# A hand-written task order replaced by another: first weight tiles, chunk steps and up-projections of a fused SSD and bilinear FFN kernel interleaved anew

## The chip, the cores and the metric

The kernel runs on one core of a Trainium2 chip. The metric is the device time of one execution in microseconds; lower is better. Before the change three runs took 272.69, 273.26 and 274.73 us, a median of 273.26. Engine names in profile rows: PE is TensorE's matmuls and PEld its weight loads, DVE is VectorE, ACT is ScalarE, POOL is GpSimd, SP is SyncE, whose queue (SPq) issues the DMA transfers.

## The reference

Two stages follow each other. The first is a chunked state-space scan over 4 batches, 8 heads, 768 positions, head size 32 and state size 16; the second is a bilinear feed-forward network on its 3072 output rows of 256.

```python
for c in range(nc):                       # chunks along the sequence
    cum = np.cumsum(la, axis=-1)          # la = log(clip(a))
    L = np.exp(cum[..., :, None] - cum[..., None, :]) * causal
    M = np.einsum('bhin,bhjn->bhij', Cc, Bc) * L
    y = np.einsum('bhij,bhjd->bhid', M, xc) \
      + np.einsum('bhin,bhnd->bhid', Cc, state) * np.exp(cum)[..., None]
    state = exp(sum(la)) * state + sum_j(B_j x_j * exp(cum_last - cum_j))
...
a = x @ w1; b = x @ w2                    # x: 3072 x 256, w1, w2: 256 x 1024
h = (a * b) @ w3                          # w3: 1024 x 1024
out = h @ w_out                           # w_out: 1024 x 256
```

The weights and inputs are 64-bit floats in memory; the kernel reads them as pairs of 32-bit words.

## The kernel before, in words

The kernel cuts the sequence into 16 chunks of 48 positions. It forms w3 @ w_out once (1024 x 256, the tile `wo`), so that the network is two up-projections, their product, and one down-projection. Every operand of a large matmul is split into a high and a low half of reduced precision, and three matmuls (high by high, high by low, low by high) stand for one.

Nothing is scheduled by a compiler. A string, PLAN (L25), is the order of all 986 tasks, and the program is emitted by walking it: each word is a task's name, an engine letter behind a colon where there is a choice (V is DVE, S is ACT, G is POOL, D is the SP queue), and behind an @ the PSUM banks (there are eight) that it writes. Each engine runs its own tasks in the order in which they stand in the string, and waits where an operand is not there or a buffer is not free. So the order of two tasks of one engine, the choice of engine and the choice of banks are all that PLAN sets. `+8@7` means eight matmuls on zeros into bank 7.

The tasks, by name:

- `t.*`, `a.*`, `k.*`, `j.*`: the decays. `t.D` and `a.D` load log-decay inputs, `t.clip`, `t.ln`, `a.clip`, `a.ln`, `a.scan`, `a.hi`, `a.lo` work them up, `a.save` writes the running sums to DRAM (tile `cq`), `k.D1` and `k.D2` load constants (tile `gs`, from in_Bt), `k.L`, `k.R0`, `k.R1` cast them into the matmul operands `ld` and `rd`, `j.m` is a small matmul.
- `cN.X`, `cN.N`, `cN.B`, `cN.K`: the loads of chunk N: its x, its B, its B and C laid out for the matmul (tile `bc`), and from chunk 2 on its running sums (`ld<-cq`, `rd<-cq`). 
- `cN.Y0`, `cN.Y1` (chunks 0 and 1 alone) build decay operands from `k.D1` and `t.D`; `cN.D0`, `cN.D1` are the decay matmuls (three matmuls each in chunks 0 and 1, one each in chunks 2 to 7; later chunks use `F` and `G` steps on DVE or POOL instead); `E0`, `E1` their exponentials on ACT; `W0`, `W1` a product on POOL.
- `cN.CB` (L352): 32 small matmuls (`ps<-bc`), C by B. `cN.M0`, `cN.M1` multiply them by the decays on DVE (`r<-ps,r`), two banks each. `cN.MX` (L366): 64 small matmuls (`ps<-r,xe`), the chunk's output and next state at once. `cN.T` (L380) transposes the state on DVE (tile `z`), eight copies `cN.Z0` to `cN.Z7` carry it into the next chunk's operand `xe`, and `cN.hi`, `cN.lo` write the output as high and low half (tile `xT`), which the up-projections read. So chunk N+1's MX waits for all of chunk N's Z.
- `wJ.*`, `vHK.*`, `oJ.*`: weight tiles: J of w1 and w2 together, of w3 transposed, of w_out. `D` loads into one of four buffers `st`, `A` (ACT), `L` and `S` (DVE) make 32-bit floats out of the 64-bit ones (`mag`), `H` casts the high half and `P` subtracts to get the low half (L424 to L461). `vHK.M` is 12 matmuls toward `wo`, `eHI.a` and `eHI.b` copy `wo` out.
- `lS.F.m`: the up-projection of rows slice S (slices of 384, 384, 512, 512, 512, 512, 256 columns) for weight tile F: 12 matmuls into two banks; `a` copies the first bank (ACT), `g` multiplies by the second (DVE), `h` and `l` split the product. `dS.T.m`: 24 matmuls of the down-projection, `y` copies them out, `x` stores them.

Slice 0 needs chunks 0 and 1, slice 1 chunks 2 and 3, and so on, so the scan and the network are interleaved on PE. Helper lines that appear in the profile: all matmuls have L136, all loads L139, two-operand DVE and POOL work L142, copies L148, activations L151.

Of the kernel before, what the change touches and what calls it, by code (L numbers as in the profile page):

```python
# [33 lines left out]
l0.6.m@6,7 c2.Z4:S c2.Z3:G c3.M1:V w7.A:S v00.D c2.Z7:G c3.M0:V o0.D c2.Z5:G c2.Z6:G l0.5.g:V l0.6.a:S c2.Z2:V w7.L:V w1.A:S l0.4.m@0,4 c6.N w1.L:V
c4.N w7.S:V c2.Z1:V c5.B w7.H:S w1.S:V l0.4.a:S w7.P:G l0.6.g:V v10.D c3.MX@2,3 l0.4.g:V o1.D c4.D0@5 a.keep c3.hi:S c3.T:V c4.D1@6 w1.H:V l0.7.m@1,0
c4.E0:S c3.Z6:G c3.lo:V c3.Z1:S w1.P:G v00.A:S c4.E1:S c3.Z7:S c3.Z5:V c3.Z2:S c3.Z0:G l1.1.m@7,4 c3.Z4:S v00.L:V c3.Z3:S o0.L:V o0.A:S c5.K v00.S:V
l0.7.a:S c4.W1:G l1.1.a:S l0.7.g:V c4.W0:G l0.1.m@5,2 v00.H:S l1.1.g:V v00.P:V l0.1.a:S o0.S:V v10.A:S v10.L:V v01.D c4.CB@0,1,6,7 l0.1.g:V l1.6.m@3,4
o0.H:S v10.S:V o0.P:G c4.M0:V v10.H:S c6.B c4.M1:V o1.A:S v11.D v02.D l1.6.a:S o1.L:V c5.D0@5 c5.D1@2 v10.P:G c5.X l1.6.g:V c4.MX@0,1 c5.E0:S c6.K
c5.E1:S c5.CB@3,4,6,7 c4.hi:S c4.T:V c5.W0:G l1.4.m@5,2 c4.lo:V c5.W1:G c6.X c5.M0:V v01.A:S c7.B c5.M1:V v01.L:V l1.4.a:S o1.S:V c9.K l1.0.m@0,1
v01.S:V o1.H:S l1.4.g:V l1.0.a:S o1.P:V v11.A:S v11.L:V l1.3.m@3,4 v01.H:V v11.S:V l1.3.a:S v01.P:V v13.D v11.H:S v02.L:V l1.5.m@6,7 c4.Z6:S v12.D  # L40
c4.Z1:G l1.0.g:V c4.Z3:S c4.Z4:G o2.D l1.3.g:V c4.Z5:S v11.P:G v02.A:S c7.N c8.K l1.5.a:S c4.Z7:V c6.D1@5 c4.Z0:V l1.7.m@2,0 c4.Z2:V c6.E1:S c8.N
v02.S:V c6.W1:G l1.5.g:V l1.7.a:S c9.F0:V v04.D c9.F1:V c5.MX@3,4 c9.G0:G l1.7.g:V c6.CB@1,2,5,6 c5.hi:S c5.T:V c7.X l1.2.m@7,0 v13.A:S c5.Z7:V c8.B
c5.Z2:G c5.lo:V c5.Z3:G c5.Z6:S c6.M1:V c5.Z4:S c9.G1:G c5.Z5:S c5.Z0:S v12.A:S v12.L:V c6.D0@3 v13.L:V c5.Z1:S v00.M@4,5,-1,-1 l1.2.a:S c7.K v12.S:V
c6.E0:S v13.S:V o2.A:S v10.M@6,7,-1,-1 c6.W0:G l1.2.g:V v02.H:S c6.M0:V v02.P:V v03.D c6.MX@0,1 c8.F0:V v05.D v12.H:V v01.M@4,5,-1,-1 c9.N c6.hi:S
o2.L:V c6.hj:S v12.P:V c6.lo:V v04.A:S c8.X o2.S:V l2.6.m@3,2 v13.H:V o3.D o2.H:V v13.P:V l2.6.a:S o2.P:V v04.L:V v02.M@4,5,-1,-1 c8.G0:V v04.S:V
c8.E0:S v03.A:S c8.W0:G c6.T:V v06.D v11.M@6,7,-1,-1 l2.6.g:V c6.Z4:G c6.Z2:S c6.Z1:S c6.Z7:G c6.lp:V c6.Z3:G v03.L:V v05.A:S l2.0.m@3,2 v05.L:V
v03.S:V v05.S:V v03.H:S v07.D v04.H:V l2.0.a:S v14.D v03.P:V v04.P:V v03.M@4,5,-1,-1 o3.A:S o3.L:V c6.Z5:V o3.S:V v12.M@6,7,-1,-1 c8.F1:V v17.D
v06.A:S v06.L:V o3.H:V v06.S:V v04.M@4,5,-1,-1 v05.H:S o3.P:V v16.D v07.A:S v07.L:V v13.M@6,7,-1,-1 v05.P:V v07.S:V v14.A:S v14.L:V v15.D
v05.M@4,5,-1,-1 c8.G1:V v06.H:S v14.S:V v07.H:S c8.E1:S v06.P:V c7.D1@0 l2.1.m@1,3 v14.H:S c10.K c8.W1:G l2.0.g:V c7.E1:S v14.P:G v17.A:S c11.N
v16.A:S v07.P:V l2.1.a:S c7.W1:G v06.M@4,5,-1,-1 l2.1.g:V v15.A:S v16.L:V v15.L:V v14.M@6,7,-1,-1 c6.Z6:V v15.S:V c10.F1:G v15.H:S v07.M@4,5,-1,-1  # L50
v15.P:V c6.Z0:V v16.S:V l2.5.m@2,0 e01.a:S@5 v17.L:V e00.a:S@4 v16.H:V v17.S:V l2.5.a:S v16.P:V v17.H:S e00.b:V@4 v17.P:G c7.D0@1 v15.M@6,7,-1,-1
e01.b:V@5 c7.E0:S l2.5.g:V c7.W0:G c7.CB@1,2,3,4 c10.G1:V c10.N v16.M@6,7,-1,-1 c10.F0:V c9.B c7.M0:V c10.G0:G c7.M1:V c7.MX@0,1 c8.CB@2,3,4,5 c9.E0:S
c7.T:V c9.X v17.M@6,7,-1,-1 c9.E1:S c7.Z7:V c10.B c7.Z1:G c8.M0:V c7.Z3:S c9.W0:G c11.K c7.Z6:S c8.M1:V c7.Z0:G c7.Z5:S c7.Z2:S c7.Z4:G c7.hi:S
c9.W1:G l2.3.m@2,3 e10.a:S@6 l0.3.h:V c12.N l0.5.h:V e11.a:S@7 l0.3.l:G c7.lo:V l0.6.h:S e10.b:V@6 l1.0.h:S l0.1.h:V l0.2.h:S l0.5.l:V l0.7.h:S
l0.2.l:G e11.b:V@7 l2.7.m@4,5 l2.3.a:S l2.3.g:V l0.7.l:G l2.7.a:S l1.0.l:V l0.1.l:V l2.4.m@0,1 l1.2.h:V c11.F0:V l1.2.l:G l2.7.g:V l2.4.a:S l0.0.h:V
c11.G0:G l2.2.m@6,7 l2.4.g:V l0.0.l:G l0.6.l:V l2.2.a:S c11.F1:V l0.4.h:V c9.CB@2,3,4,5 l1.1.h:V l0.4.l:V c8.MX@0,1 c11.B c9.M1:V d0.1.m@6 l1.1.l:V
c10.E0:S c10.X c8.T:V c10.E1:S c10.W0:G l2.2.g:V c8.Z2:S c8.Z7:G c12.K c8.Z4:S c10.W1:G c9.M0:V c8.Z1:S c8.Z0:G c8.Z5:S c13.N c8.hi:S c8.Z6:V c8.Z3:V
c11.G1:V c8.lo:V c10.CB@2,3,4,5 d0.1.y:V c9.MX@0,1 c10.M1:V c12.B d0.1.x c10.M0:V d0.2.m@7 c11.E1:S c11.X c9.T:V c11.E0:S c11.W1:G c9.Z7:S c9.Z6:V
c13.K c9.Z0:G c9.hi:S c9.hj:S c9.Z2:V c9.Z5:G c9.lo:V c9.lp:V c9.Z3:G c9.Z1:V c9.Z4:G c12.F0:G c10.MX@4,5 d0.2.y:V d0.2.x c11.CB@0,1,2,3 c11.W0:G
c10.hi:S c10.T:V c12.X c12.G0:G l3.7.m@6,7 c10.Z4:S c10.lo:V c13.B c10.Z1:S c10.Z0:S c11.M1:V c14.N c10.Z3:G c12.E0:S c11.M0:V c10.Z5:G c12.W0:G  # L60
l3.7.a:S c10.Z2:V c12.F1:G l3.1.m@4,5 c10.Z6:V c12.G1:G l3.7.g:V c10.Z7:V c12.E1:S c13.F0:G l3.1.a:S c14.K c13.F1:G c11.MX@2,3 l3.1.g:V c12.CB@0,1,6,7
# [611 lines left out]
```

## Time and profile before

| | before |
|---|---|
| median of 3 runs | 273.26 us |
| profiled execution | 273.01 us |
| span of its instructions | 270.8 us |
| PE busy | 264.0 us, 97% |
| DVE busy | 173.0 us, 64% |
| ACT busy | 115.6 us, 43% |
| POOL busy | 81.5 us, 30% |
| matmuls, weight loads | 3022 each |
| DMA moved | 33.94 MB, mean 125 GB/s, 200 to 330 GB/s in most of the first 75 us |

Times in profile rows are microseconds from the first instruction of the span; the last number in a row of groups is the mean of one instruction in ns. A row of the timeline gives start, length, engine, line, operation, destination and source, how many were merged, and in brackets the idle time before it and what ended it. Lengths of neighbouring matmuls overlap, since they are pipelined. "issue" is idle time for which the profile shows no cause.

### The profile page before, as it was taken

The numbers are of one execution on the slowest core, as the hardware profiler recorded it, in microseconds if no ns is written. First come the engines' busy times: TensorE is split into PE (matmuls) and PEld (weight loads), VectorE is DVE, ScalarE is ACT, GpSimd is POOL, SyncE is SP. The second block draws the span as 40 slices with busy tenths as digits, with TensorE's granted clock in tenths as the row PEclk, the third lists the DMA queues.
The fourth block names the chain that finished last, engine by engine and source line by source line (L and its number), as shares of the span: only waits on it lengthen the run. The fifth ranks groups of instructions, "written<-read, shape, count | busy, mean of one in ns | idle before, by whom it ended". The sixth has DMA issues, their size and how long they took to land.

```text
span 270.8 us, 7391 instructions
## 1 busy us (share of the span) xinstructions
PE 264.0 (97%) x3022; PEld 231.8 (86%) x3022; DVE 173.0 (64%) x347; ACT 115.6 (43%) x253; POOL 81.5 (30%) x120
## 2 busy tenths in 40 slices
...
GB/s 196 333 312 239 315 295 185 295 291 280 295 289 181 2 189 47 85 267 161 136 43 21 39 22 39 39 2 90 41 41 19 22 1 39 23 19 22 39 19 41
DMA packets 21754, 33.94 MB, mean 125 GB/s; under 512 B 3672, under 2 KB 13528, under 8 KB 21720
## 3 DMA queue, kind: packets, MB, share of 16 engines
...
q8 instruction: 24, 0.39, 0.6%
...
## 4 chain that ended last, share of the span: by engine, by line
PE 96%; issue 1%; ACT 1%; DVE 1%; DVEq 0%; ACTq 0%
PE ps L136 96%; DVE xT L142 0%; ACT xT L148 0%; DVE xe L148 0%; ACT ob L148 0%; ACT r L151 0%; ACT xe L148 0%; DVE zero L224 0%; DVE z L382 0%; DVEq L382 0%; ACTq L148 0%
## 5 line engine op out<-in xcount | busy, mean ns | idle before, releaser
L136 PE MATMUL ps<-xT,wh 128*128 128x512 f32 (+2 forms) x448 | 124.3, 361 | 0.3 <-DVE xT L142 0.3
L136 PEld LDWEIGHTS ps<-xT,wh 128*128 128x128 f32 x448 | 79.9, 188 | 10.6 <-issue 0.6
L136 PE MATMUL ps<-xT,wl 128*128 128x512 f32 (+2 forms) x224 | 80.5, 359 | 0.0
L136 PE MATMUL ps<-wo,fr 128*128 128x256 f32 x576 | 70.0, 281 | 0.0
L136 PEld LDWEIGHTS ps<-wo,fr 128*128 128x128 f32 x576 | 68.8, 189 | 0.8
L142 DVE TENSOR_TENSOR gs<-gs,ps 128x512 f32<-128x512 f32 (+2 forms) x56 | 33.5, 605 | 35.3 <-PE ps L136 33.1
L142 POOL TENSOR_TENSOR fr<-gs,fr 128x512 fp32r<-128x512 f32 (+2 forms) x19 | 23.8, 1258 | 91.8 <-PE ps L136 42.2
L136 PEld LDWEIGHTS ps<-xT,wl 128*128 128x128 f32 x224 | 42.2, 188 | 5.4 <-POOL wl L142 0.3
L148 ACT COPY gs<-ps 128x512 f32<-128x512 f32 (+2 forms) x56 | 29.1, 524 | 40.3 <-PE ps L136 40.0
L142 DVE TENSOR_TENSOR fr<-gs,fr 128x512 fp32r<-128x512 f32 (+2 forms) x37 | 26.0, 729 | 0.8 <-ACT fr L148 0.5
L142 POOL TENSOR_TENSOR r<-bn,r 128x128 f32<-128x128 f32 x32 | 14.9, 473 | 36.8 <-ACT r L151 19.8
L136 PE MATMUL ps<-fr 128*128 128x256 f32 x192 | 24.8, 285 | 0.7 <-issue 0.7
L136 PEld LDWEIGHTS ps<-fr 128*128 128x128 f32 x192 | 23.9, 191 | 1.5 <-issue 0.9
L148 ACT COPY ob<-ps 128x256 f32<-128x256 f32 x14 | 5.2, 373 | 44.9 <-PE ps L136 44.9
L148 DVE CAST fr<-gs 128x512 fp32r<-128x512 f32 (+2 forms) x30 | 13.3, 469 | 16.6 <-PE ps L136 16.6
L148 ACT CAST fr<-gs 128x512 fp32r<-128x512 f32 (+2 forms) x26 | 13.4, 557 | 17.6 <-PE ps L136 13.0
L151 ACT ACTIVATE mag<-st 128x512 f32<-128x512 f32 x28 | 18.8, 677 | 2.0 <-DMA st<-in_w_dram 1.6
L450 DVE SCALAR_TENSOR_TENSOR mag<-mag,st 128x512 uint32<-128x512 uint32 x28 | 18.8, 684 | 0.6 <-ACT mag L151 0.3
L148 POOL COPY xe<-z 16x128 f32<-16x128 f32 x36 | 11.9, 331 | 21.1 <-DVE z L382 8.8
L148 ACT COPY xe<-z 16x128 f32<-16x128 f32 x52 | 15.4, 296 | 3.1 <-DVE z L382 1.1
L142 DVE TENSOR_TENSOR r<-ps,r 128x384 f32<-128x384 f32 x32 | 16.4, 546 | 0.3 <-PE ps L136 0.2
L136 PEld LDWEIGHTS ps<-r,xe 64*32 64x32 f32 x1024 | 11.5, 105 | 5.3 <-issue 2.9
...
## 6 DMA issues: line engine op xcount, KB each, us to landing
...
```

The lines of the kernel that those rows point to most:

```text
L136: pin(nc.tensor.matmul(*args, **kw))
L142: pin((nc.gpsimd if e == "G" else nc.vector).tensor_tensor(*args))
L148: pin(nc.scalar.copy(*args) if e == "S" else (nc.gpsimd if e == "G" else nc.vector).tensor_copy(*args))
L151: pin(nc.scalar.activation(*args, **kw))
L450: pin(nc.vector.scalar_tensor_tensor(d, m, 3, v["wl"].bitcast(U32), ALU.logical_shift_left, ALU.bitwise_or))
```

## The change

PLAN is replaced as a whole by another order of the same tasks. The functions, the sizes, the loops and every matmul stay. The number of zero matmuls goes from 20 (8, 3, 8, 1) to 18 (8, 1, 3, 6). The tasks on DVE go from 347 to 327, on ACT from 253 to 265, on POOL from 115 to 123.

At the start, the order of the loads was a, c0.B, t, k.D1, c0.X, k.D2, w2, c0.N, c1.B, a.save, c1.N, w0, c1.X, w3, c2.B, ...; it becomes t, k.D1, a, c0.X, c0.B, c0.N, w0, c1.X, k.D2, c1.N, a.save, c1.B, w2, w1, c2.K, c2.X, w7, w6, c3.N, w4, c2.B, ... The four Y builds, three of which were on POOL, are all on DVE. c1.D1 and j.m go behind c0.MX, c2.CB goes from ahead of the first up-projection to behind the fourth. The up-projections of slice 0 take the weight tiles in the order 0, 2, 1, 7, 6, 4, 3, 5 instead of 0, 2, 3, 5, 6, 4, 7, 1. Further on, the MX and CB runs, the v products, the up- and the down-projections are interleaved in another order and with other banks. The diff, cut to its beginning and to the stretch around c5.MX:

```diff
@@ -23,63 +23,63 @@
 PLAN = """
-k.act:S k.zero:V k.keep:G a.D +8@7 c0.B t.D k.D1:D c0.X k.D2:D a.clip:V a.ln:S w2.D a.scan:V c0.N a.hi:V c0.CB@0,1,2,3 a.lo:V c1.B t.clip:V +3@7
-t.ln:S a.save k.R0:V k.L:S c1.N c0.Y0:G w0.D j.m@4 k.R1:S c1.Y1:V c1.X c0.D0@5 c0.Y1:G w2.A:S w2.L:V w3.D c0.D1@6 c1.Y0:G c0.E0:S c2.B w2.S:V c1.D0@7
-c0.E1:S c2.N c0.W0:G j.c:V w2.H:S c0.W1:G c0.M0:V c2.K c1.D1@5 w2.P:G c1.E0:S c0.M1:V c0.MX@0,1 c1.W0:G c1.E1:S w0.A:S w0.L:V w5.D c1.CB@2,3,6,7
-c1.W1:G c0.T:V +8@4 c0.hi:S w0.S:V c0.Z7:S c0.Z4:S c0.Z0:G c1.M1:V c0.Z6:S c0.Z5:G c0.Z2:S c1.M0:V c0.Z3:S c0.Z1:V w0.H:V c1.MX@4,5 w3.A:S c2.X
-c0.lo:V c3.N w0.P:V +1@1 c1.hi:S c2.CB@2,3,6,7 w6.D c1.T:V c1.lo:V c2.D0@0 w4.D w3.L:V c2.D1@1 l0.0.m@4,5 c2.E0:S w3.S:V c3.K c2.E1:S c2.W0:G w3.H:V
-l0.0.a:S c2.W1:G c2.M0:V w5.A:S w3.P:G c2.M1:V l0.2.m@0,1 c5.N c1.Z0:S l0.0.g:V c1.Z2:S c3.B c1.Z5:S c1.Z3:S c1.Z6:V c1.Z7:S w5.L:V c1.Z4:S w5.S:V
-c1.Z1:S l0.2.a:S l0.3.m@4,2 w6.L:V c3.X w6.A:S w5.H:V w7.D l0.2.g:V w5.P:G l0.3.a:S w4.A:S w1.D c2.MX@6,7 l0.3.g:V w4.L:V c3.D1@3 c4.B c2.hi:S w6.S:V
...
+t.D k.zero:V k.act:S +8@7 k.D1:D a.D c0.X t.clip:V c0.B c0.N w0.D t.ln:S k.R0:S k.keep:G k.L:V c0.Y0:V +1@7 c0.D0@0 a.clip:V a.ln:S c1.X k.D2:D c1.N
+a.scan:V c0.Y1:V +3@7 c1.Y0:V a.hi:S a.lo:V c1.Y1:V c0.D1@1 a.save c0.E0:S c1.B c0.CB@2,3,4,5 c0.W0:G c1.D0@6 c0.E1:S w0.A:S c1.E0:S k.R1:S w2.D
+c0.W1:G c0.M0:V w1.D c0.M1:V c1.W0:G w0.L:V c0.MX@0,1 c1.D1@7 w0.S:V c1.CB@2,3,4,5 c0.T:V c2.K c0.hi:S c0.Z5:V c0.Z0:G c0.Z3:G c1.E1:S c0.Z7:V c0.lo:V
+c0.Z6:V +6@7 c2.X c0.Z4:G c1.W1:G w0.H:S c0.Z2:S w7.D c1.M0:V c0.Z1:V c1.M1:V w2.A:S c1.MX@0,1 j.m@6 w0.P:V w2.L:V c1.T:V c1.hi:S c2.D0@7 c1.lo:V
+w2.S:V w1.A:S w1.L:V w2.H:S w2.P:V c2.D1@2 j.c:S c2.E0:S c1.Z5:S w1.S:V w7.L:V l0.0.m@3,4 w7.A:S w1.H:S w7.S:V l0.2.m@5,0 w1.P:V l0.2.a:S w6.D w6.A:S
+c1.Z3:S w7.H:S c1.Z0:S l0.1.m@1,6 w6.L:V l0.2.g:V c3.N w6.S:V w7.P:V w4.D l0.0.a:S c2.B c2.N l0.7.m@7,5 w4.A:S l0.1.a:S c1.Z2:G c2.E1:S w3.D c3.K c3.B
+w6.H:V w4.L:V c2.CB@0,1,2,3 w6.P:G l0.0.g:V c1.Z1:G c1.Z6:G c2.W1:G c2.W0:G l0.7.a:S c1.Z4:S w4.S:V l0.1.g:V w5.D c3.X l0.7.g:V c2.M1:V c2.M0:V w4.H:S
+w3.A:S c4.B o0.D l0.6.m@4,7 c1.Z7:S w4.P:G w3.L:V w3.S:V w3.H:V w5.L:V c2.MX@5,6 c3.D1@3 c3.D0@2 c2.T:V c3.E1:S c2.hi:S l0.6.a:S c3.E0:S l0.4.m@0,1
+c2.lo:V c4.K w3.P:G l0.6.g:V c2.Z4:S c4.X v10.D c3.CB@2,3,4,5 c3.W0:G c3.W1:G c2.Z1:G c2.Z2:G w5.A:S c2.Z7:S c2.Z6:S l0.4.a:S o0.A:S c2.Z5:S c3.M1:V
...
+o1.S:V c6.B l1.2.g:V c4.Z0:S c4.Z3:S c4.Z1:S c6.E0:S l1.0.a:S l1.3.m@7,3 l1.3.a:S v00.H:S c6.W1:G c8.G1:G c5.M0:V c4.Z2:V c4.Z6:G c6.W0:G l1.0.g:V
+l1.3.g:V c5.MX@0,1 c5.hi:S c6.X v01.D c7.K c9.K v04.D c5.T:V v01.L:V c6.CB@4,5,6,7 c6.M0:V c6.M1:V v10.M@2,3,-1,-1 v13.P:G v03.D l1.6.m@4,5 c5.Z0:V
+o1.H:S c5.Z2:S v00.P:V c5.lo:V v02.D c5.Z1:V v12.H:V v01.A:S c7.D0@6 v11.M@2,3,-1,-1 c5.Z4:S v04.A:S l1.6.a:S c8.F0:V v12.P:V v01.S:V o1.P:V v04.L:V
...
 """
```

PE's whole order, new, from the first up-projection to the first down-projection (engine words and banks left out):

```
l0.0 l0.2 l0.1 l0.7 c2.CB l0.6 c2.MX c3.D1 c3.D0 l0.4 c3.CB l0.3 c4.D1 c3.MX c4.D0 l0.5 l1.5 c4.CB
c5.D0 l1.1 c5.D1 l1.7 l1.4 c4.MX c5.CB l1.2 c6.D0 c6.D1 l1.0 l1.3 c5.MX c6.CB v10 l1.6 c7.D0 v11 c7.D1
v00 v12 c6.MX v13 v01 l2.5 l2.2 l2.6 v02 l2.3 v03 c7.CB v04 l2.0 v14 c7.MX v05 v15 v06 c8.CB v16 v07 v17
l2.1 l2.4 l2.7 c8.MX c9.CB d0.1 d0.0
```

and old:

```
l0.0 l0.2 l0.3 c2.MX c3.D1 c3.D0 l0.5 c3.CB l0.6 l0.4 c3.MX c4.D0 c4.D1 l0.7 l1.1 l0.1 c4.CB l1.6 c5.D0
c5.D1 c4.MX c5.CB l1.4 l1.0 l1.3 l1.5 c6.D1 l1.7 c5.MX c6.CB l1.2 c6.D0 v00 v10 c6.MX v01 l2.6 v02 v11
l2.0 v03 v12 v04 v13 v05 c7.D1 l2.1 v06 v14 v07 l2.5 c7.D0 v15 c7.CB v16 c7.MX c8.CB v17 l2.3 l2.7 l2.4
l2.2 c9.CB c8.MX d0.1 c10.CB c9.MX d0.2
```

95 lines of the change are left out of this document (45 added, 50 removed).

## The prediction

> **What bounds it now.** I read the page first (busy shares, chain), then what TensorE waited for, the chain in order of time, TensorE's timeline, and the other engines' timelines of the first 20 us.
>
> ```profile
> span 270.8 us, 7391 instructions
> PE 264.0 (97%) x3022; PEld 231.8 (86%) x3022; DVE 173.0 (64%) x347; ACT 115.6 (43%) x253; POOL 81.5 (30%) x120
> ...
> q8 instruction: 24, 0.39, 0.6%
> ...
> PE 96%; issue 1%; ACT 1%; DVE 1%; DVEq 0%; ACTq 0%
> ```
>
> TensorE (PE) is busy for 97% of the span and holds 96% of the chain that ends last. In all it waits 3.0 us, and half of that is two gaps that no instruction explains ("issue"):
>
> ```profile
> PE ps L136 <- issue: 1.3, 2, 0.7
> PE ps L136 <- DVE zero L224: 1.2, 1, 1.2
> PE ps L136 <- DVE xT L142: 0.3, 1, 0.3
> PE ps L136 <- DVE xe L148: 0.2, 1, 0.2
> ```
>
> The chain in order of time (start, length, what) says where the stream of matmuls is closed:
>
> ```profile
> 19.49 42.66 PE ps L136 x548
> 62.15 0.66 issue
> ...
> 119.57 147.27 PE ps L136 x1383
> ```
>
> So the time is the sum of three things: when the first up-projection (l0.0.m) starts, 19.49; the TensorE stream from there to its end at 119.57 + 147.27 = 266.84, which is 247.35; and what follows, 270.8 - 266.84 = 4.0 inside the span and 273.01 - 270.8 = 2.2 outside it. No matmul is added but zero matmuls (20 before, 18 after), which only fill waits. So the change can act through the start, through the waits in the stream, and through the cost of changing from one shape to another.
>
> **The stream, step by step.** TensorE's timeline gives the prices; these are starts, and I take differences of starts, since the printed durations overlap:
>
> ```profile
> 12.60 0.86 PE L136 MATMUL ps<-r,xe 64*32 64x64 f32 x64
> 13.39 0.59 PE L136 MATMUL ps<-bc 32*64 32x96 f32 x32
> 13.91 1.90 PE L136 MATMUL ps<-zero 128*128 128x512 bf16 x8
> ...
> 25.30 0.51 PE L136 MATMUL ps<-xT,wh 128*128 128x384 f32 x2
> 25.64 0.34 PE L136 MATMUL ps<-xT,wl 128*128 128x384 f32 x1
> 25.91 0.86 PE L136 MATMUL ps<-r,xe 64*32 64x64 f32 x64
> ...
> 61.03 1.12 PE L136 MATMUL ps<-fr 128*128 128x256 f32 x8
> 62.80 2.17 PE L136 MATMUL ps<-fr 128*128 128x256 f32 x16 [0.66 <-issue]
> 64.90 0.86 PE L136 MATMUL ps<-r,xe 64*32 64x64 f32 x64
> ...
> 119.04 0.32 PE L136 MATMUL ps<-r,xe 64*32 64x64 f32 x8
> ...
> 120.29 0.59 PE L136 MATMUL ps<-bc 32*64 32x96 f32 x32
> ```
>
> An MX run (64 small matmuls) takes 13.39 - 12.60 = 0.79, a CB run (32) 13.91 - 13.39 = 0.52. Going from large matmuls into such a run costs 25.91 - 25.64 less the 0.17 that one 384-column matmul takes (two from 25.30 to 25.64), 0.10, and I take as much for going out: 0.2 for each stretch of small runs.
> What the stream lost: the sixteen 128x256 matmuls from 62.80 to 64.90 cost 0.125 each with the change of shape in it, so the eight from 61.03 should have taken 1.0 and took 1.77: 0.8 lost. The MX run from 119.04 took 1.25 to 120.29: 0.46 lost to a late carry. Without both the old stream is 247.35 - 0.8 - 0.46 = 246.1.
> The new order has c2.CB behind l0.0.m, where the old one had done it before: +0.52. From l0.0.m on I count 19 stretches of small runs where there were 17: +0.4. New stream without waits: 247.0.
>
> **The start.** These rows carry it:
>
> ```profile
> 2.11 0.43 SPq L139 DMA_DIRECT2D gs<-in_Bt_dram  x1
> 6.19 0.33 SPq L139 DMA_DIRECT2D cq<-cp  x1
> 11.54 0.38 SPq L139 DMA_DIRECT2D ld<-cq  x1
> ```
>
> ```profile
> 2.80 0.26 DVE L145 TENSOR_SCALAR gs<-gs 128x192 f32<-128x192 f32 x1 [1.67 <-DMA gs<-in_a_dram]
> 4.73 0.28 DVE L145 TENSOR_SCALAR la<-la 128x256 f32<-128x256 f32 x1
> 6.13 0.55 DVE L148 CAST rd<-gs 64x768 fp32r<-64x768 f32 x1 [1.12 <-DMA gs<-in_Bt_dram]
> 6.61 1.18 DVE L142 TENSOR_TENSOR gs<-la,gs 128x384 f32<-128x384 f32 x1
> 11.16 1.02 DVE L142 TENSOR_TENSOR r<-ps,r 128x384 f32<-128x384 f32 x2
> 13.50 0.45 DVE L382 STREAM_TRANSPOSE z<-ps 128x256 f32<-128x256 f32 x1
> 15.48 0.22 DVE L148 COPY xe<-z 16x128 f32<-16x128 f32 x1
> 18.82 0.52 DVE L142 TENSOR_TENSOR xT<-ps,xT 128x384 fp32r<-128x384 f32 x1
> ```
>
> ```profile
> 4.71 0.65 PEld L136 LDWEIGHTS ps<-bc 32*64 32x64 f32 x32 [0.84 <-DMA bc<-in_c_dram]
> ```
>
> Old: all four decay steps of chunks 0 and 1 run ahead of c0.MX, which starts at 12.60. New: c1.D1 goes behind c0.MX, but all four Y builds move to VectorE (DVE), where one takes 1.18; three were on GpSimd. They need k.D1. It was fourth in the queue, issued at 2.11 and landed by 6.13; it becomes second. The first transfer took 0.73 to 2.80; the old second one (c0.B, larger) was issued at 1.18 and landed by 4.71. So k.D1 lands between 3.3 (1.18 + 2.07) and 5.2 (1.18 + its own 4.02); I take 4.1, between the two rows that are second or first in the queue.
> DVE's order from there: k.L 0.25, four Y 4.72, the a-chain clip to lo (2.80 to 4.73 is 1.93 with a cast that now goes to ScalarE, so 1.65), two M 1.02. End 4.1 + 0.25 + 4.72 + 1.65 + 1.02 = 11.74: c0.MX at 11.8, 0.8 earlier than 12.60. TensorE is ready: eight zeros to 4.7, then D0, zeros, D1, CB and c1.D0 at 1.2, 0.7, 1.2, 0.5 and 1.2 from about 5.6, so 10.8 or so.
> From the end of c0.MX at 12.6 DVE runs T 0.45, four carries of 0.25, lo 0.52 and two M of 0.51, 3.0 with their hops 0.1: c1.MX at 15.75, which the six zeros wait for. In the old run it started at 15.74, waited for a carry, then stalled:
>
> ```profile
> 15.74 1.15 PE L136 MATMUL ps<-r,xe 64*32 64x64 f32 x60
> 17.52 0.30 PE L136 MATMUL ps<-r,xe 64*32 64x64 f32 x4 [0.63 <-issue]
> ```
>
> and ended at 17.52 + 4 x 0.06 = 17.75 instead of 16.55. From its end to the end of the lo copy (18.82 + 0.52) was 1.60. The new plan does the same three copies, so lo ends at 16.55 + 1.60 = 18.15. Old l0.0.m used banks 4 and 5, in which c1.MX had just written, so its first matmul waited for lo; new l0.0.m has banks 3 and 4 and c1.MX 0 and 1, so only its second matmul does. It starts as if at 18.0, j.m and the two c2.D being done by 17.6. **Gain at the start 1.5.** Bounds: k.D1 at its ends shifts it by -0.8 or +1.1.
>
> **Waits in the new stream.** The weights are prepared as they were, mostly on DVE, now in the order w0, w2, w1, w7, w6, w4, w3, w5:
>
> ```profile
> L450 DVE SCALAR_TENSOR_TENSOR mag<-mag,st 128x512 uint32<-128x512 uint32 x28 | 18.8, 684 | 0.6 <-ACT mag L151 0.3
> ...
> 70.00:80.00 10.00, 10.00 (x74) 9.50 (x73) 9.94 (x23) 6.29 (x12) 1.38 (x4) 1.00 0.88 305
> ...
> 110.00:120.00 10.00, 9.75 (x294) 8.53 (x295) 9.24 (x23) 4.26 (x12) 4.27 (x12) 1.00 0.68 194
> ```
>
> With 0.68 for each S, as much for P, about 0.45 for L, and one l0 product, DVE finishes w7's low half some 6.2 to 6.9 after 18.15, at 24.4 to 25.0; l0.7.m wants it after 36 + 2 matmuls of 0.17, at 18.0 + 6.6 = 24.6. I take 0.2 of wait (bounds 0 and 0.5). Behind that DVE was the tight engine: 9.94 of 10 us at 70 to 80 (third pair of columns in the window rows). The new plan gives it 327 tasks instead of 347 (GpSimd and ScalarE take them), and adding its tasks up in order from l0.0.m its work lies 1.2 to 8 us ahead of TensorE's at every step, where the old order had it up to 1.5 behind. I found no bank that is read too late by more than a few tenths: 0.
>
> Then the issue gaps. The page counts 24 transfers on q8 for 3022 matmuls and as many weight loads: one for 252 instructions, 126 matmuls. By the program's order the gaps lie ahead of matmuls 221 and 852, 631 = 5 x 126 apart. I read them as waits for the next piece of program. The piece that ended at the first had run 3.9 us, that at the second 6.4, both while the DMA engines were about full; two pieces of 4.5 us between 110 and 120, where their share is 0.68, show no gap. In the new order c1.MX again ends such a piece (4.4 us), and two pieces of about 6.2 us lie near 29 to 35 and 54 to 60. Bounds: 0, and three gaps of 0.8, 2.4; I take 0.8, one such gap, because the pieces are as short as those that stalled but fewer transfers are queued at 29 to 35, where SP waits for buffers.
> The Trainium skill (Runtime: NRT & Kernel Launch, Instruction fetch mechanics) says that programs are fetched in blocks of 256 instructions and that the cost of crossing into one is mostly hidden. The size agrees with 252; the trace's 0.63 and 0.66 do not look hidden. By the rule the term would be 0 and the time 0.8 lower.
>
> **Sum.** 18.0 + 247.0 + 0.2 + 0.8 = 266.0 against 266.84: 0.8 less. The tail after the last matmul is the same two copies and stores. The profiled execution's 273.01 becomes 272.2; the median of the runs, 273.26, is 0.25 above it, so I say 272.4.
>
> **Rivals.**
> A. The spreading works fully: no gap, k.D1 early. 272.4 - 0.8 - 0.8 - 0.2 = 270.6. For it: the gaps are real and sit where dense runs meet. Against: three short pieces remain.
> B. Slower: c2.K is late. a.save now waits for the a-chain behind three Y builds, to about 9.5 instead of 6.19, and SP takes things in order, so c1.B, w2, w1 and c2.K queue behind it. c2.K reads what a.save wrote; in the old run its first part went out 11.54 - 6.19 = 5.35 after it. With that, and as long again to land, c2.K is there at 9.5 + 5.35 + 5.35 = 20.2; c2.D0 stands ahead of l0.0.m on TensorE, so everything moves 2.2: 274.6. It decides as soon as c2.K lands after 17.6. Against: at 9.5 little else is queued, and two transfers at the first one's 2.07 with 1.4 of issuing land by 15.1.
> C. The spreading does nothing: all three short pieces stall, 2.4 instead of 0.8. 274.0. For it: the new pieces are no longer than the old.
> D. The clock turns over later. Eight zeros took 3.60 at the start, and 1.90 in the row of 13.91:
>
> ```profile
> 1.19 3.60 PE L136 MATMUL ps<-zero 128*128 128x512 bf16 x8 [1.19 <-DVE zero L224]
> ```
>
> so TensorE ran at half rate at first, and was at full by c0.D0 in the old run. If Y0 is late (k.D1 at 5.2), TensorE idles from 5.1 to 6.6 and may stay at half for D1, CB and c1.D0, 2.9 us more, of which DVE's later end hides about half: 1.1 + 1.4 against the forecast, 274.9. The Trainium skill (TensorE: Matmul & The Clock Gate, Part 1) puts the turn after a busy window of about 3.4 us; by that rule the idle stretch would cost one more window.
>
> **Chances.** Forecast 0.50, A 0.18, B 0.12, C 0.10, D 0.10. The measurement tells about 1% (2.7 us) from no change. Most of A and a tail of the forecast fall near or under 270.5: faster 0.18. B, C and D each alone stay within 1%; two of them together, or a wait in the stream that I missed, pass 276.0: slower 0.14. Same 0.68. The range, meant to hold 8 times in 10, is 269.8 (A with another 0.8 found) to 275.9 (D and C's half together); the forecast's own is 271.2 to 273.7.
>
> **What would show it.** Right: c0.MX near 11.8, the first 128x384 up matmul near 18.0, the issue gaps down to about one, PE still 97%. Wrong: the first up matmul after 19, which says k.D1 or c2.K was late (the weight load that waits names it); or PE waits above 3 us after 20, which says that DVE or a bank was late; or issue gaps of 2 us.

## The result

The changed kernel takes 270.9 us (median of 19 runs, 269.18 to 274.75), against 273.76 us for the kernel before in the same series; the ratio is 0.9916, with a 95% interval of 0.9892 to 0.994. The ratios compare the runs outside the slower state alone, so they are not the quotients of the medians. So the changed kernel is faster by 0.8%, some 2.3 us (1.6 to 3.0). The forecast was 272.4, a change of less than 1%. The sign and the wide range (269.8 to 275.9) held, but the gain is some 2.7 times what was forecast (0.86), and the time lies under the forecast's own range (271.2 to 273.7).

The profiled execution took 271.64. Its page, in the lines that answer to those shown of before:

```profile
span 269.6 us, 7353 instructions
...
PE 262.9 (98%) x3020; PEld 231.1 (86%) x3020; DVE 162.4 (60%) x327; ACT 120.0 (44%) x265; POOL 89.3 (33%) x128
...
q8 instruction: 23, 0.38, 0.6%
...
PE 90%; DVE 3%; DMA 2%; ACT 2%; issue 1%; POOL 1%; SPq 0%; POOLq 0%; ACTq 0%; DVEq 0%
```

What TensorE waited for:

```profile
PE ps L136 <- DVE zero L224: 1.2, 1, 1.2
PE ps L136 <- issue: 0.9, 1, 0.9
PE ps L136 <- DVE fr L142: 0.5, 1, 0.5
```

The chain in order of time:

```profile
12.35 2.77 PE ps L136 x75
...
15.46 1.14 issue
...
18.21 12.45 PE ps L136 x145
...
79.81 185.78 PE ps L136 x1899
```

The last matmul ends at 79.81 + 185.78 = 265.59 instead of 266.84. There is still an issue gap of 0.9, now in the last matmul of c1.MX, and a new wait of 0.5 for DVE at 79. TensorE's timeline of the start (the third matmul of l0.0.m is the row of 18.49; before, it was that of 19.92):

```profile
5.14 0.68 PE L136 MATMUL ps<-rd,ld 48*128 48x384 f32 x1
...
10.23 0.89 PE L136 MATMUL ps<-r,xe 64*32 64x64 f32 x64
...
14.30 1.10 PE L136 MATMUL ps<-r,xe 64*32 64x64 f32 x63
16.29 0.21 PE L136 MATMUL ps<-r,xe 64*32 64x64 f32 x1 [0.89 <-issue]
...
18.49 0.34 PE L136 MATMUL ps<-xT,wl 128*128 128x384 f32 x1
```

c0.MX runs at 10.23, where 11.8 had been forecast. VectorE's timeline tells why: k.D1 had landed by 3.5, a Y takes 0.5 here, not 1.18, and ahead of the two M (the row of 9.20) VectorE waits 2.09 for TensorE.

```profile
3.54 0.22 DVE L148 CAST ld<-gs 96x128 fp32r<-96x128 f32 x1 [0.46 <-DMA gs<-in_Bt_dram]
3.68 0.55 DVE L142 TENSOR_TENSOR gs<-la,gs 128x384 f32<-128x384 f32 x1
4.15 0.25 DVE L145 TENSOR_SCALAR gs<-gs 128x192 f32<-128x192 f32 x1
...
5.37 1.00 DVE L142 TENSOR_TENSOR gs<-la,gs 128x384 f32<-128x384 f32 x2
...
9.20 1.02 DVE L142 TENSOR_TENSOR r<-ps,r 128x384 f32<-128x384 f32 x2 [2.09 <-PE ps L136]
```

In the sum's own terms, against the same execution of before: the start is 18.49 - 19.92 = 1.43 earlier, the stream from there to the last matmul 247.10 instead of 246.92, 0.18 longer. Forecast were 1.5 earlier and 0.65 longer.

### The profile page after: what moved, and what is told of

It reads as the page before. It is cut to its first block, busy times and chain, and to the rows that moved or that the text cites. A ratio compares the mean times of both kernels' runs of the same rounds, so it can differ in the third digit from the quotient of the medians.

```text
span 269.6 us, 7353 instructions
## 1 busy us (share of the span) xinstructions
PE 262.9 (98%) x3020; PEld 231.1 (86%) x3020; DVE 162.4 (60%) x327; ACT 120.0 (44%) x265; POOL 89.3 (33%) x128
## 4 chain that ended last, share of the span: by engine, by line
PE 90%; DVE 3%; DMA 2%; ACT 2%; issue 1%; POOL 1%; SPq 0%; POOLq 0%; ACTq 0%; DVEq 0%
PE ps L136 90%; DMA xe<-in_x_dram 2%; POOL fr L142 1%; DVE mag L450 1%; DVE fr L142 0%; DVE st L145 0%; ACT r L151 0%; DVE z L382 0%; ACT mag L151 0%; ACT ob L148 0%; ACT fr L148 0%; DVE gs L142 0%; DVE xT L142 0%; ACT xT L148 0%; ACT gs L148 0%
## 5 line engine op out<-in xcount | busy, mean ns | idle before, releaser
L142 POOL TENSOR_TENSOR fr<-gs,fr 128x512 fp32r<-128x512 f32 (+2 forms) x26 | 30.6, 1193 | 69.5 <-PE ps L136 39.7
L148 ACT CAST fr<-gs 128x512 fp32r<-128x512 f32 (+2 forms) x33 | 18.0, 564 | 39.2 <-PE ps L136 28.4
L142 DVE TENSOR_TENSOR fr<-gs,fr 128x512 fp32r<-128x512 f32 (+2 forms) x30 | 19.9, 687 | 9.1 <-ACT fr L148 8.8
L142 DVE TENSOR_TENSOR r<-ps,r 128x384 f32<-128x384 f32 x32 | 17.1, 551 | 10.2 <-PE ps L136 9.2
L450 DVE SCALAR_TENSOR_TENSOR mag<-mag,st 128x512 uint32<-128x512 uint32 x28 | 20.8, 745 | 1.5 <-ACT mag L151 0.8
L148 DVE CAST fr<-gs 128x512 fp32r<-128x512 f32 (+2 forms) x23 | 12.5, 560 | 12.1 <-issue 8.4
L148 ACT COPY xe<-z 16x128 f32<-16x128 f32 x51 | 15.1, 296 | 6.0 <-DVE z L382 4.5
L148 POOL COPY xe<-z 16x128 f32<-16x128 f32 x33 | 10.3, 312 | 19.0 <-issue 8.7
L142 POOL TENSOR_TENSOR fr<-mag,fr 128x512 fp32r<-128x512 f32 x8 | 11.1, 1384 | 14.0 <-ACT fr L148 11.5
L148 DVE COPY ob<-ps 128x256 f32<-128x256 f32 x8 | 3.4, 422 | 19.6 <-PE ps L136 16.4
```

Of the source, the lines that this page charges most:

```text
L142: pin((nc.gpsimd if e == "G" else nc.vector).tensor_tensor(*args))
L148: pin(nc.scalar.copy(*args) if e == "S" else (nc.gpsimd if e == "G" else nc.vector).tensor_copy(*args))
L450: pin(nc.vector.scalar_tensor_tensor(d, m, 3, v["wl"].bitcast(U32), ALU.logical_shift_left, ALU.bitwise_or))
```

## The experiments

The theory with which I went in: the gain is the earlier start; what varies is the issue gap, which is a wait for the next piece of TensorE's program on q8. Rivals: the gap is chance or belongs to c1.MX; the gain lies in the stream's order; the loads bound the start whatever TensorE does. The ratios are to the kernel before, timed beside each. Starts and ends are those in the profiled execution. The diffs show only the words around what moves, out of longer lines.

| kernel | c0.MX | third matmul of l0.0.m | last matmul ends | median | ratio to before |
|---|---|---|---|---|---|
| before, first profile | 12.60 | 19.92 | 266.84 | 273.26 | |
| before again | 12.53 | 20.43 | 266.13 | 272.38 | 0.9982 (0.9949 to 1.0016) |
| before, new start alone | 11.30 | 20.24 | 268.22 | 273.94 | 1.0019 (0.9987 to 1.005) |
| changed, first profile | 10.23 | 18.49 | 265.59 | 270.9 | 0.9916 (0.9892 to 0.994) |
| changed again | 9.86 | 17.21 | 264.45 | 270.61 | 0.9926 (0.9893 to 0.9959) |
| no zeros ahead of c1.MX | 9.47 | 17.73 | 264.25 | 271.54 | 0.9962 (0.9929 to 0.9996) |
| c1.B early | 10.85 | 18.76 | 265.39 | 271.75 | 0.9962 (0.993 to 0.9994) |
| both | 9.75 | 17.91 | 265.89 | 272.36 | 0.9978 (0.9948 to 1.0008) |
| three Y on GpSimd | 9.36 | 17.42 | 264.36 | 272.58 | 0.998 (0.9944 to 1.0015) |
| k.D1 fourth | 13.13 | 20.27 | 268.54 | 274.5 | 1.0033 (0.9998 to 1.0067) |
| c1.D1 ahead of c0.MX | 10.88 | 18.52 | 265.67 | 272.03 | 0.996 (0.9932 to 0.9987) |
| c7.X early | 10.60 | 18.34 | 266.72 | 271.56 | 0.9951 (0.9919 to 0.9982) |
| three waits moved | 10.44 | 18.66 | 266.51 | 270.9 | 0.9918 (0.989 to 0.9947) |
| j.m ahead, c7.X early | 10.00 | 17.16 | 264.20 | 270.91 | 0.9918 (0.9887 to 0.995) |

### The changed kernel again

> The changed kernel unaltered, for a second profile and as the yardstick of the three beside it. My theory of the issue gap in chunk 1's mixing run (c1.MX): the next piece of TensorE's program, fetched on q8, had landed only at 15.0, and TensorE goes on about 1.3 us after that, at 16.3. That depends on the DMA load alone, so the gap should come again, between 0.5 and 1.2, at the last matmul of c1.MX, and the wait at the second matmul of v02 (0.5 to 0.9) too. The median should be 0.8 to 1.0% under the kernel before. Rival: the gap is a chance event of the one profiled execution; then it is absent, and the start is 0.9 earlier than 18.2.

It took 270.61. TensorE's timeline shows no issue gap at all, and the start is 1.3 earlier than in the first profile (17.21 against 18.49):

```profile
9.86 0.89 PE L136 MATMUL ps<-r,xe 64*32 64x64 f32 x64
...
14.05 1.15 PE L136 MATMUL ps<-r,xe 64*32 64x64 f32 x64
...
16.40 0.62 PE L136 MATMUL ps<-rd,ld 96*128 96x384 f32 x2 [0.56 <-DMA ld<-cq]
...
17.21 0.34 PE L136 MATMUL ps<-xT,wl 128*128 128x384 f32 x1
```

So the gap need not come: what I had expected of it fell, the rival's "absent" is right. But its place is no chance. In the trace's records of q8 the piece that c1.MX's last matmul needs landed at 15.0 in the first execution and at 13.6 in this one; the matmul ran at 16.29, 1.3 behind the landing, and at 15.0, 1.4 behind it. The DMA view of the first execution between 13.8 and 15.05 has that one transfer; between 15.1 and 16.3 it has none on q8:

```profile
q8 instruction: 1, 0.02, 5.7%
```

Next late here is c2.K (`ld<-cq`), 0.56, and one weight at l0.7.m.

### The kernel before again

> The kernel before, unaltered, for a second profile. Fetch theory: each piece of TensorE's program is fetched after the piece ahead of it was entered, and TensorE needs it landed about 1.5 earlier; so an issue gap shows only at a boundary whose piece landed less than 1.7 ahead, and those boundaries keep their place (matmul 221 and every 126 behind it) whatever the gap does. I expect the first up-projection at 19.0 to 19.8, and one or two gaps of 0.4 to 1, among the boundaries near 17.5, 62 and 120. Rival (chance): gaps at places that are no boundaries.

TensorE's timeline has a gap of 1.20 in c1.MX again, none at 62 (the 24 matmuls of 61.56 run in 3.04, 0.127 each), and this row ahead of the first decay matmul:

```profile
7.09 0.67 PE L136 MATMUL ps<-la,gs 128*128 128x256 f32 x2 [1.18 <-DMA gs<-in_Bt_dram]
...
18.04 0.30 PE L136 MATMUL ps<-r,xe 64*32 64x64 f32 x4 [1.20 <-issue]
```

```profile
61.56 3.04 PE L136 MATMUL ps<-fr 128*128 128x256 f32 x24
```

j.m waits for k.D2, and the decay matmuls behind it run back to back from 7.69 to c0.MX at 12.53: in the old order a load sets the start. The gap at 62 that the forecast counted as a loss of the old stream is there in one execution of two, and so is the late carry at 119. The piece of program behind the gap landed at 61.3 in the first and at 57.7 in this one.

Over all 14 profiled executions of this study the records show 322 such boundaries, from matmul 221 on one every 126. TensorE has nine issue gaps in them, of 0.4 to 1.8, and all nine stand within two matmuls of a boundary whose piece had landed only 1.3 to 1.7 before TensorE went on. The count places a boundary no better than to two matmuls: at matmul 851 TensorE stopped one or two matmuls behind the count, and in one execution the matmul at the count ran 0.7 ahead of the landing. Allowing for that, at no boundary did TensorE go on less than 1.27 behind the landing. So the reading of the gaps as waits for the program is borne out. Whether a given boundary is hit varies from run to run with how late the fetch is: it started between 2.8 ahead of the entry into the piece before it and 5.5 behind that (1.8 to 5.5 behind at the nine gaps), and took 0.9 to 1.9. What makes it late is not shown.

### The zeros and c1.B

```diff
-c0.Z6:V +6@7 c2.X
+c0.Z6:V c2.X
```

> The changed kernel without the six zero matmuls ahead of c1.MX. Fetch theory: the boundary of a piece of program stands at a fixed count of matmuls, so it falls six matmuls later, ahead of the second matmul of l0.0.m, when the piece has long landed. The gap in c1.MX is gone, its 64 matmuls take 0.8 instead of 2.2, c1.T starts near 15.4 instead of 16.6, and the second matmul of l0.0.m near 17.1 instead of 18.2; the time falls by 0.5 to 1.1 (w7 or c2.K may take some of it back). Rival 1, the gap is no fetch but something that c1.MX itself waits for: it stays at 0.9 in the same place, 0.0. Rival 2, the zeros keep the clock up: without them TensorE is idle for 1.4 us ahead of c1.MX, its matmuls and those of the next 3 us take twice their time, and the kernel is 1 to 2 us slower.

```diff
-c1.X k.D2:D c1.N
+c1.B c1.X k.D2:D c1.N
...
-c0.E0:S c1.B c0.CB@2,3,4,5
+c0.E0:S c0.CB@2,3,4,5
```

> The changed kernel with the load of chunk 1's B and C (c1.B) ahead of c1.X in the queue instead of behind a.save. It landed at 12.30 and c1.CB waited 0.63 for it; now it lands by 11, so c1.CB and with it c1.M and c1.MX could start 0.5 earlier. Fetch theory: nothing is gained, since the piece of program still lands near 15.0 and the last matmul of c1.MX still waits for it until 16.3; the gap grows from 0.9 to about 1.4. Rival, the gap is a stall of fixed length or something of c1.MX's own: the whole start moves 0.5 earlier and the gap stays 0.9.

> Both edits: no zeros ahead of c1.MX, and c1.B early. Fetch theory: now c1.B's 0.5 is worth its length, so 0.5 more than the kernel without the zeros alone, 1.0 to 1.6 less than the changed kernel, unless c2.K (landed at 16.0) or the weights set the start then: the second matmul of l0.0.m near 16.7. Rival (no fetch): 0.5 less than the changed kernel, the same as c1.B early alone. Rival (clock): slower than the changed kernel.

None came out faster than the changed kernel. By the ratios they lie 0.4 to 0.6% above it, with intervals that overlap that of the changed kernel timed beside them. Without the zeros the gap in c1.MX is gone, as the fetch theory has it; but it was gone in the second execution of the changed kernel too, so its absence here proves nothing. Rival 2 came true beside it. TensorE is idle for 1.15 ahead of c1.MX (its timeline), and the windows (TensorE's busy time, then those of the others; the granted clock is the third number from the end) show the price:

```profile
13.71 0.27 PE L136 MATMUL ps<-r,xe 64*32 64x64 f32 x2 [1.15 <-DMA st<-in_w_dram]
```

```profile
14.00:15.00 1.00, 0.66 (x48) 0.66 (x50) 1.00 (x3) 0.59 (x1) 0.00 (x0) 0.69 0.87 268
15.00:16.00 1.00, 1.00 (x35) 0.76 (x22) 0.62 (x2) 0.09 (x1) 0.00 (x0) 0.50 0.81 266
16.00:17.00 1.00, 1.00 (x4) 0.89 (x3) 0.45 (x2) 0.91 (x2) 0.28 (x1) 0.50 0.87 274
17.00:18.00 1.00, 1.00 (x5) 0.90 (x5) 1.00 (x3) 0.35 (x2) 0.00 (x0) 0.61 0.98 337
```

The shortfall is 0.31 + 0.50 + 0.50 + 0.39 = 1.7, so some 3.4 us at half clock (an estimate, twice the shortfall). The third matmul of l0.0.m comes at 17.73, 0.5 behind the execution of the changed kernel that had no gap, though c0.MX was 0.4 ahead of it. With c1.B early alone its wait went, which had been only 0.1 to 0.2 on TensorE and not the 0.63 of the expectation; but in that execution TensorE ran at half rate until about 7.1, so c0.MX was late at 10.85, and no gap came, since the piece had landed at 14.1: my expectation of a longer gap was not tested, and the time speaks against any gain. With both, the idle time was 1.58, the clock fell again, and a gap stood at the boundary of 63.72 (TensorE's timeline):

```profile
63.72 1.22 PE L136 MATMUL ps<-fr 128*128 128x256 f32 x8 [1.07 <-issue]
```

That is the boundary of the old kernel's gap at 62, in the new order. The new order does not do away with it.

### What brought the start forward

The first try at the parts undoes, in the changed kernel, the choice of engine for three Y:

```diff
-k.L:V c0.Y0:V
+k.L:V c0.Y0:G
...
-a.scan:V c0.Y1:V
+a.scan:V c0.Y1:G
...
-c1.Y0:V a.hi:S
+c1.Y0:G a.hi:S
```

> The changed kernel with three of its four Y builds back on GpSimd (c0.Y0, c0.Y1, c1.Y0), c1.Y1 left on VectorE. The prediction had priced a Y at 1.18 on VectorE, from one that ran while GpSimd did the same; in the changed kernel, with GpSimd idle, it took 0.5. Theory 1 (sharing, and TensorE bounds the start): on GpSimd they take 0.9 to 1.0 each, c1.Y1 on VectorE takes more than 0.8 if it overlaps one of them, and the time stays within 0.4 of the changed kernel, since all four are done before TensorE's own chain (zeros, D0, D1, CB, c1.D0) wants them: c0.MX between 9.5 and 11. Theory 2 (the move to VectorE is what brought the start forward): c0.MX near 12, the first up-projection and the end about 1.2 later.

Rows of GpSimd, VectorE and TensorE:

```profile
3.66 2.67 POOL L142 TENSOR_TENSOR gs<-la,gs 128x384 f32<-128x384 f32 x3 [2.52 <-ACT la L151]
```

```profile
3.83 0.78 DVE L145 TENSOR_SCALAR gs<-gs 128x192 f32<-128x192 f32 x1
```

```profile
9.36 0.89 PE L136 MATMUL ps<-r,xe 64*32 64x64 f32 x64
```

A Y takes 0.9 on GpSimd, and VectorE's clip beside it 0.78, against 0.25 (row of 4.15) in the changed kernel, where GpSimd was idle: VectorE is held up beside it. The 1.18 has the same company: in the old kernel that Y ran from 6.61 to 7.79, GpSimd's three Y from 6.25 to 9.27. c0.MX is not later for it, so theory 2 falls: the engine of the Y does not set the start. The time is another matter: 272.58, 0.5% above the changed kernel by the ratios (the intervals of the two timed side by side just overlap), where I had expected 0.4 us at most. The profiled execution ends its matmuls with the changed kernel's second profile (264.36 and 264.45). Behind them its span runs on for 5.3, against 4.0 in each of the other 13 executions: the last output stores are done at 268.9 instead of 267.6. Nothing in the trace ties that to the Y, and whether it comes again is not known; the loss stays open.

```diff
-k.D1:D a.D c0.X t.clip:V
+a.D c0.X k.D1:D t.clip:V
```

> The changed kernel with k.D1 fourth in the load queue as before, instead of second. Theory 1 (the early k.D1 is what brought the start forward): the first Y is built near 5.9 instead of 3.7, c0.D0 runs near 6.8 instead of 5.1, c0.MX near 11.5 to 12 instead of 9.9 to 10.2, and the second matmul of l0.0.m near 18.7 to 19.3; the time is 0.8 to 1.8 more than that of the changed kernel. Rival (the weights' loads bound the start whatever TensorE does): the matmuls of l0.0.m start later, but a wait for the weights in l0.2.m to l0.7.m, 0.5 in the second profile, goes away in exchange; then at most 0.5 more.

This one decides. 274.5, 1.1% above the changed kernel by the ratios, so more than the whole gain is lost with the place of one load. TensorE's timeline:

```profile
6.47 0.69 PE L136 MATMUL ps<-rd,ld 48*128 48x384 f32 x1 [1.26 <-DVE gs L145]
...
8.53 1.49 PE L136 MATMUL ps<-zero 128*128 128x512 bf16 x3
9.95 0.69 PE L136 MATMUL ps<-rd,ld 48*128 48x384 f32 x1
...
13.13 0.89 PE L136 MATMUL ps<-r,xe 64*32 64x64 f32 x64
```

Y0 is built at 5.73 instead of 3.68, TensorE idles 1.26, and then three zeros take 1.49 instead of 0.81 and a decay matmul 0.69 instead of 0.44: half rate until about 10.5, though the granted clock is given as 1.00 there. c0.MX comes at 13.13, later than in the old kernel. That is the prediction's rival D, with its own mechanism. The matmuls end 3.0 to 4.1 later than in the two profiles of the changed kernel; 1.8 to 3.1 of that is the start, and a wait of 0.55 for GpSimd at 103.3 is half of the rest.

The reverse, the kernel before with the early loads, the Y on VectorE, c0.CB behind c0.D1 and j.m behind c0.MX, but with the rest of its order:

```diff
-k.act:S k.zero:V k.keep:G a.D +8@7 c0.B t.D k.D1:D c0.X k.D2:D a.clip:V
+t.D k.zero:V k.act:S k.keep:G +8@7 k.D1:D a.D c0.X t.clip:V c0.B c0.N t.ln:S k.R0:S k.L:V c0.Y0:V c0.D0@5 a.clip:V
...
-c0.M1:V c0.MX@0,1 c1.W0:G
+c0.M1:V c0.MX@0,1 j.m@4 j.c:V c1.W0:G
```

> The kernel before with the start alone of the change: t.D and k.D1 first in the load queue, the four Y builds on VectorE, j.m behind chunk 0's mixing run instead of ahead of c0.D0. Its stream from l0.0.m on, with c2.CB ahead of it and c1.D1 ahead of c0.MX, is the old one. Theory (the start is the whole gain): c0.D0 runs near 4.6 to 5.2 instead of 7.7, c0.MX near 10.8 to 11.4 instead of 12.5, the first up-projection 1 to 2 earlier than 19.5 to 20.0, and the time falls by 0.4 to 0.8% (1.0 to 2.2), near to that of the changed kernel. Rival 1 (the gain lies in the new order of the stream): not more than 0.2% faster. Rival 2 (the loads of the weights bound the old stream's start): c0.MX is early, but the matmuls of l0.2.m to l0.5.m wait for a weight by what was won.

No gain: 1.0019. c0.MX came 1.2 earlier, as expected, and then c1.MX was late. TensorE, VectorE, then ScalarE and GpSimd:

```profile
11.30 0.30 PE L136 MATMUL ps<-r,xe 64*32 64x64 f32 x2
...
16.44 0.27 PE L136 MATMUL ps<-r,xe 64*32 64x64 f32 x2 [0.80 <-POOL xe L148]
16.96 1.20 PE L136 MATMUL ps<-r,xe 64*32 64x64 f32 x62 [0.25 <-ACT xe L148]
```

```profile
13.27 0.42 DVE L148 COPY la<-ps 128x256 f32<-128x256 f32 x1 [1.56 <-PE ps L136]
13.99 0.43 DVE L145 TENSOR_SCALAR st<-st 128x512 uint32<-128x512 uint32 x1 [0.29 <-DMA st<-in_w_dram]
14.33 0.44 DVE L382 STREAM_TRANSPOSE z<-ps 128x256 f32<-128x256 f32 x1
...
15.32 1.01 DVE L142 TENSOR_TENSOR r<-ps,r 128x384 f32<-128x384 f32 x2
```

```profile
15.37 1.54 ACT L148 COPY xe<-z 16x128 f32<-16x128 f32 x5
```

```profile
15.14 0.76 POOL L148 COPY xe<-z 16x128 f32<-16x128 f32 x2 [1.74 <-DMA xe<-in_x_dram]
```

In this order VectorE has j.c (13.27) and w0.L (13.99) ahead of c0.T (14.33). It waits for j.m, which the edit put behind c0.MX, and then for the load of w0. So c0.T comes 1.8 behind the end of c0.MX (12.53), where the changed kernel has 0.3 (11.31 against 11.05). The two M of chunk 1 end at 16.33 and ScalarE's carries at 16.91, and they release c1.MX at 16.44 and 16.96. GpSimd, which the row of 16.44 names, was done by 15.9. The load of w0 is issued at 8.18 here, at 7.19 in the old kernel, where it was there by 13.0 and c0.MX ended only at 13.39, and at 3.54 in the changed kernel. c1.X is late too (issued at 9.20, landed at 15.0; 4.53 and 9.6 in the changed kernel), but here it set nothing: GpSimd's carries, which waited for it, were done before the M. So the theory that the start alone brings the whole gain fell, in the form of this edit: k.D1 is needed, but an early k.D1 pays nothing while j.c and w0 hold up VectorE behind c0.MX. That w0 and c1.X early beside it would bring the rest was not tried by itself. Nor does this run test rival 1 (the gain lies in the stream's order), since l0.0.m did not start earlier. (This execution also lost 1.75 to a gap at 64.24, the same boundary again.)

```diff
-c0.MX@0,1 c1.D1@7
+c1.D1@7 c0.MX@0,1
```

> The changed kernel with c1.D1 ahead of c0.MX again, as before the change. Theory (TensorE's own chain sets the start): c0.MX comes 1.2 later (10.6 to 12), VectorE's work behind it moves along, c1.MX starts 0.8 to 1.2 later (14.9 to 16.4), and the second matmul of l0.0.m at 17.8 to 19.2; the time is 0.4 to 1.0 more than that of the changed kernel. Rival (the loads bound the start): c1.CB had waited 0.2 to 0.8 for c1.B and l0.7.m 0.5 for a weight, so the step costs at most 0.3.

c0.MX is 1.2 behind its place by c0.D0 (4.87 to 10.88, against 5.07 to 9.86 in the changed kernel's second profile), yet the third matmul of l0.0.m is at 18.52, level with the changed kernel's first profile. TensorE's timeline shows why:

```profile
16.32 0.21 PE L136 MATMUL ps<-r,xe 64*32 64x64 f32 x1 [0.45 <-issue]
```

The piece of program had landed at 15.0 in both, and the last matmul of c1.MX ran at 16.32 and 16.29: what came later was taken from the gap. The time, 0.996, lies 0.3 to 0.4% over the changed kernel with overlapping intervals: not settled.

### A version that beats both?

```diff
-v02.D c5.Z1:V
+v02.D c7.X c5.Z1:V
...
-c8.X c7.X
+c8.X
```

> The changed kernel with the load c7.X directly behind v02.D in the queue, and no longer behind c8.X. In the traces VectorE waits 0.9 for it ahead of a carry (c6.Z5), behind which stand the steps that make v02's high and low halves, and the matmuls of v02 wait 0.2 to 0.75. Theory: c7.X lands some 5 earlier, the wait at the carry and that at v02 go (v02 takes 1.45 instead of 1.65 to 2.2), and the time falls by 0.2 to 0.7. Rival: the wait only moves to the next late thing on VectorE or to v02.D's own landing, and the time stays within 0.2.

```diff
-c2.D0@7 c1.lo:V
+c1.lo:V
...
-w2.P:V c2.D1@2 j.c:S c2.E0:S c1.Z5:S w1.S:V w7.L:V l0.0.m@3,4 w7.A:S w1.H:S
+w2.P:V j.c:S c1.Z5:S w1.S:V w7.L:V l0.0.m@3,4 c2.D0@7 c2.D1@2 w7.A:S w1.H:S c2.E0:S
...
-w5.P:V v13.D l0.5.m@0,6
+w5.P:V l0.5.m@0,6
...
-c5.K c4.N
+c5.K v13.D c4.N
```

> The changed kernel with three moves against waits that the profiles show: c2.D0 and c2.D1 behind l0.0.m instead of ahead of it (they waited up to 0.56 for c2.K), the load v13.D behind c5.K (c5.D0 waited 1.28 for c5.K in one profile), and c7.X behind v02.D (the wait of 0.2 to 0.75 at v02). Theory: all three waits are gone in its profile, nothing above 0.4 takes their place except at a boundary of the program's pieces or at l0.7.m's weight (0.5), and the time is 0.2 to 1.0 less than the changed kernel's, 0.9 to 1.2% under the kernel before. Rival: the loads and the fetches that vary from run to run put other waits in their place, and the time is that of the changed kernel within 0.2%.

(c7.X is early in this one and in the next as well.)

```diff
-c0.Z6:V +6@7 c2.X
+c0.Z6:V +3@7 c2.X
...
-c1.MX@0,1 j.m@6
+j.m@6 c1.MX@0,1
```

> The changed kernel with j.m ahead of c1.MX and three zero matmuls there instead of six: TensorE stays busy as long ahead of c1.MX, but one matmul fewer stands ahead of its end. And c7.X behind v02.D again, which took the wait at v02 away. Fetch theory: the boundary now falls right behind c1.MX, ahead of c2.D0, so all 64 matmuls of c1.MX run without an issue gap (64 in 0.8 to 1.3, c1.T near 15.4); the matmul that stands behind the boundary still comes no earlier than 1.3 behind the landing of its piece (near 16.3 if that lands near 15.0), and the second matmul of l0.0.m near 17.0 to 17.3 instead of 18.2 in the runs that had a gap. No wait at v02. The time is 0.3 to 1.0 less than the changed kernel's, 0.9 to 1.3% under the kernel before. Rival, the gap is not tied to the count of matmuls: it stays at the last matmul of c1.MX. Rival (what is saved at the start is lost to late loads further on): the time is that of the changed kernel.

The wait at v02 in the changed kernel is told by VectorE's row and TensorE's:

```profile
73.92 0.22 DVE L148 COPY xe<-z 16x128 f32<-16x128 f32 x1 [0.92 <-DMA xe<-in_x_dram]
```

```profile
79.81 1.46 PE L136 MATMUL ps<-fr 128*128 128x256 f32 x10 [0.49 <-DVE fr L142]
```

With c7.X early the carry finds its operand there, and v02 runs without a wait in all three kernels. But the time does not fall below that of the changed kernel. In the profile of c7.X early alone another load was late (TensorE):

```profile
43.19 0.44 PE L136 MATMUL ps<-rd,ld 96*128 96x384 f32 x1 [1.28 <-DMA ld<-cq]
```

Its place is ahead of the edit, so the edit did not make it. With the three moves c5.K is in time, but o1.D, a load behind it, is there only at 50.5, where the changed kernel had it at 48.8 and 48.0. VectorE waits for it, and TensorE for VectorE:

```profile
50.49 0.43 DVE L145 TENSOR_SCALAR st<-st 128x512 uint32<-128x512 uint32 x1 [2.03 <-DMA st<-in_w_out_dram]
```

```profile
51.44 0.62 PE L136 MATMUL ps<-xT,wh 128*128 128x384 f32 x2 [0.81 <-DVE gs L142]
```

That the new place of v13.D did this is not shown, since o1.D came at 50.4 with c7.X early alone. And with j.m ahead of c1.MX, TensorE busy up to it, all 64 matmuls run without an issue gap, but what waits then is c2.K (TensorE):

```profile
14.31 0.84 PE L136 MATMUL ps<-r,xe 64*32 64x64 f32 x62 [0.16 <-DVE r L142]
16.36 0.61 PE L136 MATMUL ps<-rd,ld 96*128 96x384 f32 x2 [1.21 <-DMA ld<-cq]
```

Its piece of program had landed at 13.7, early enough for either place, so this run does not test the boundary; it shows the next limit. 270.9 and 270.91 for the last two kernels: no version here beats the changed one by what can be measured.

## Why the prediction was right, and where its sizes were off

**The sign**, and that the change lies within 1%, were right, and for the reason given first: the start is earlier, and the stream from l0.0.m on costs a little more. Against the execution that the prediction used, the two profiles of the changed kernel give 1.43 and 2.71 for the start (forecast 1.5), +0.18 and +0.32 for the stream (forecast +0.65), and 1.25 and 2.39 for the end (forecast 0.8). But the second profile of the kernel before starts 0.51 later than the first and has a stream that is 1.22 shorter. Taken two against two, the start gained 2.3, the stream lost 0.9, and the matmuls end 1.5 earlier. The runs say 2.3, and 1.6 at the least; where the rest lies the profiles do not show. So the start was the term that was too small, and the stream's was about right. The gain does not lie in the stream's order.

**The stream's prices** held. Counted from the third matmul of l0.0.m, 0.43 behind the first, the forecast's old stream without waits is 245.7. The second profile of the kernel before, with neither the gap at 62 nor the late carry, has 245.70. Without the waits told below, the new one is 246.4 and 246.3, 0.6 to 0.7 longer, where 0.52 and 0.4 had been counted.

**The start: the step that failed is "DVE's order from there", four Y at 1.18.** The 1.18 was read from a Y that shared its time with one on GpSimd; alone it takes 0.5. So VectorE does not set c0.MX (it waited 2.09 for TensorE there); TensorE does, from c0.D0 on, and c0.MX came at 10.23 and 9.86 instead of 11.8. k.D1 landed by 3.5, near the early bound of 3.3. That the first profile still had the start where it was forecast (1.43 against 1.5) is luck, two errors against each other: c1.MX began 1.45 early (14.30 against 15.75), but took 2.14 instead of 0.8, and 0.89 of that is a gap that the prediction had put in the stream. In the second profile the gap is absent and the start shows its size.

**The waits in the new stream** were 1.0 in the forecast, 0.2 for w7 and 0.8 for a gap. The gap came, one of them and at c1.MX, in the first execution, and none in the second. A wait for a weight at l0.7.m was 0 and 0.5. "No bank is read too late by more than a few tenths: 0" was wrong by v02, 0.74 over its usual 1.44 in the first and 0.41 in the second: there it was no bank but c7.X, late in the load queue, which the count of tasks did not hold.

**The gaps.** That they are waits for a piece of program holds; that the new order spreads them away is not shown. The one at 62 is absent in both profiles of the changed kernel, but also in the second of the kernel before, and it is back in a kernel that has the new order. The prediction's 631 matmuls between the two gaps are 5 x 126 and one more, as the place of a boundary is known to a matmul or two. The Trainium skill (Runtime: NRT & Kernel Launch, Instruction fetch mechanics) has the crossing mostly hidden; 313 of 322 boundaries agree, and nine cost 0.4 to 1.8.

**The rivals.** A (everything works, 270.6) is nearest to the time, but for half its reasons: k.D1 early was right and was needed. B (c2.K late) has the right place and the wrong price: a.save went out at 7.02, not 9.5, c2.K landed at 16.0, and the wait is 0.56 to 1.21, and only where the start was early enough to feel it. C fell: the short pieces at 29 to 35 and 54 to 60 did not stall in either profile, though the second of them did without the zeros and with c1.B early (the gap of 63.72). D is real: by the spacing of its first matmuls TensorE went to full rate between 4.1 and 7.1 in the executions with the early k.D1, and c0.MX followed, 9.36 to 10.85; the full price showed only where TensorE idled (k.D1 fourth). The Trainium skill (TensorE: Matmul & The Clock Gate, Part 1) puts the turn after some 3.4 us of busy time; the 3.4 us at half clock behind the idle stretch without the zeros agree, while the turns at the start, 2.9 to 5.9 behind the first matmul at 1.19, spread more widely.

**What stays open**: why three Y on GpSimd cost 0.5%, and whether c1.D1's place is worth anything; both lie near what 12 runs tell apart. Open too is how the gain at the start divides between k.D1, w0 and c1.X: k.D1's place alone loses all of it, and k.D1 early alone wins none.
